# Issuing the main loop of a fused FFT-filter and MLP kernel in emission order

## The chip, the cores and the metric

The kernel runs on one core of one Trainium2 chip. The metric is the time of one execution in device microseconds (us), median of several runs. The profile is one execution taken by the hardware profiler. Engines are named as in it: PE is TensorE (PEld its weight loads), DVE VectorE, ACT ScalarE, POOL GpSimd, SP SyncE, which here does nothing but issue DMAs. The granted clock is the share of TensorE's full clock that the profile says it was given.

## The reference, cut to what matters

```python
X = np.fft.rfft(x, axis=1)                      # x: (8, 3008, 256)
y = np.fft.irfft(X * (filt_r + 1j * filt_i), n=3008, axis=1).astype(np.float32)
h = y.reshape(8 * 3008, 256) @ w_in             # (24064, 2048)
s = np.sin(alpha * h)
out = (h + s * s / (alpha + 1e-09)) @ w_out     # (24064, 256)
```

## The kernel before: the parts that matter

The Fourier filter is done per batch in three stages of small matmuls. They pass their data through DRAM tiles (d1, d2) to change its layout. Its pieces are emitted between the steps of the MLP loop by a plan, so that PE always has MLP work beside them. Loads and stores:

- stage 1: two `pa` matmuls a step, `t1` stored to d1; after the last, eight `t2` loads from d1;
- stage 2: `pb`, filter product `p`, `pc`, `g` stored to d2;
- stage 3: one `t4` load (384 KB) from d2 per chunk of four steps, then four `pd` matmuls a step, result `y`.

```python
xpool = pool("xp", 4)     # x, loaded on POOL's queue
t4pool = pool("t4", 3)
fps = pool("fps", 2, PSUM)     # pa, pb, pc, pd
hps = pool("hps", 4, PSUM)     # ph
ops = pool("ops", 2, PSUM)     # po
...
def stage3(u):                                  # u = 0..15, chunk ch = 0..3
    ch, rest = divmod(u, 4)
    half, cb = divmod(rest, 2)
    if rest == 0:
        t4 = t4pool.tile([NK, 8, C], FP16, name=f"t4_{b}_{ch}", tag="t4")
        marks["t4"] = nc.sync.dma_start(out=t4, in_=d2_rows[:, 8 * ch:8 * ch + 8, :])
        st["t4"] = t4
    ps = fps.tile([128, 4, 128], FP32, name=f"pd_{b}_{u}", tag="f")
    ...
    for i in range(4):
        nc.tensor.matmul(out=psv[:, i, :], lhsT=st["t4"][:, 4 * half + i, cb * 128:cb * 128 + 128],
                         rhs=wi_t, start=True, stop=True)                      # L219
    ...
...
plan = {1: [-45 + i for i in range(8)],
        2: [-29 + 14 * i / 13 for i in range(13)],
        3: [-10, -9] + [-7 + 2 * i for i in range(14)]}     # steps from 48 * b
...
for k in range(len(chunks) + 1):
    for j in range(8):                          # one step
        if k < len(chunks):
            hidden(k, 2 * j)                    # 2 ph matmuls (L354), sine on ACT, v on DVE
            hidden(k, 2 * j + 1)
        if k == 0:
            weights_out(j)
        while pending and pending[0][0] <= step:
            pending.pop(0)[2]()                 # the filter's pieces of this step
        if k > 0:
            n_half = 2 * (chunks[k - 1][2] // 128)
            for u in range(n_half * j // 8, n_half * (j + 1) // 8):
                project(k - 1, u)               # 8 po matmuls (L369); each 4th: ACT copies o, SP stores it
        step += 1
```

The Tile framework takes this program, finds the dependencies, and its scheduler chooses the order in which each engine's queue issues its instructions.

Of the kernel before, what the change touches and what calls it, by code (L numbers as in the profile page):

```python
# [12 lines left out]
ALU = mybir.AluOpType  # L13
# [41 lines left out]
def kernel(  # L55
# [10 lines left out]
    nc = tc.nc  # L66
# [12 lines left out]
    def behind(ins, other):  # L79

        tc.add_manual_dep(ins.ins, other.ins.name, mybir.DependencyInfo(
            mybir.DependencyClass.NoSync, mybir.DependencyReason.DATA), reason="order of work")
# [29 lines left out]
    marks = {}  # L112
# [158 lines left out]
    for g in range(4):  # L271
        for k, filt in enumerate((filt_r, filt_i)):
            for q in range(2):
                off, step = ((6 * g) * C, C) if q == 0 else ((N1 - 6 * g) * C, -C)
# [58 lines left out]
    def weights_out(i):  # L333

        if i in (2, 3, 4, 5):
            for jb in range(4 * i - 8, 4 * i - 4):
                behind(nc.vector.tensor_scalar(  # L337
                    out=w2[:, jb, :], in0=w_out32[:, jb, :], scalar1=rec_t[:, jb:jb + 1],
                    scalar2=-0.5, op0=ALU.mult, op1=ALU.mult), marks["snake"])


    chunks = [(pb, c0, min(512, 2 * S - c0)) for pb in range(B // 2) for c0 in range(0, 2 * S, 512)]
# [4 lines left out]
    def hidden(k, jb):  # L347

        _, c0, n = chunks[k]
        if jb == 0:  # L350
            v[k] = vpool.tile([128, 16, 512], FP16, name=f"v_{k}", tag="v")
        ps = hps.tile([128, 512], FP32, name=f"ph_{k}_{jb}", tag="h")
        for cb in range(2):
            nc.tensor.matmul(out=ps[:, 0:n], lhsT=w1[:, cb, jb * 128:jb * 128 + 128],  # L354
                             rhs=y_cols[:, cb, c0:c0 + n], start=(cb == 0), stop=(cb == 1))
        cs = cospool.tile([128, 512], FP32, name=f"cos_{k}_{jb}", tag="c")
        nc.scalar.activation(out=cs[:, 0:n], in_=ps[:, 0:n], func=AFT.Sin, bias=float(np.pi / 2))  # L357
        marks["snake"] = nc.vector.scalar_tensor_tensor(  # L358
            out=v[k][:, jb, 0:n], in0=cs[:, 0:n], scalar=-1.0, in1=ps[:, 0:n],
            op0=ALU.add, op1=ALU.subtract)  # L360

    def project(k, u):

        pb, c0, n = chunks[k]
        t, half = divmod(u, 2)
        if t % 2 == 0 and half == 0:
            pso[k] = ops.tile([128, 2, C], FP32, name=f"po_{k}_{t}", tag="o")
        for jb in range(8 * half, 8 * half + 8):
            nc.tensor.matmul(out=pso[k][:, t % 2, :], lhsT=v[k][:, jb, 128 * t:128 * t + 128],  # L369
                             rhs=w2[:, jb, :], start=(jb == 0), stop=(jb == 15))  # L370
        last = 128 * (t + 1) == n
        if half == 1 and (t % 2 == 1 or last):
            nb = t % 2 + 1
            o = opool.tile([128, 2, C], FP32, name=f"o_{k}_{t}", tag="o")
            nc.scalar.copy(out=o[:, 0:nb, :], in_=pso[k][:, 0:nb, :])  # L375
            for i in range(nb):
                store(o[:, i, :], pb, c0 + 128 * (t + 1 - nb + i))

    def store(o_blk, pb, col):

        p = 0
        while p < 128:
            odd, rest = divmod(col + p, S)
            n2, row = divmod(rest, NR)
            cnt = min(128 - p, NR - row)
            t0 = (2 * pb + odd) * S + 32 * row + n2
            nc.sync.dma_start(
                out=bass.AP(tensor=out.tensor, offset=out.offset + t0 * C,
                            ap=[[32 * C, cnt], [1, C]]),
                in_=o_blk[p:p + cnt, :])  # L390
            p += cnt
# [7 lines left out]
    pending = [(1 + i % 4 + 8 * (i // 4), 0, piece) for i, (_, piece) in enumerate(first[25:])]  # L399
# [7 lines left out]
            pending.append((at_step, b, piece))  # L407
    pending.sort(key=lambda p: p[0])
    step = 0
    for k in range(len(chunks) + 1):  # L410
        for j in range(8):
            if k < len(chunks):
                hidden(k, 2 * j)
                hidden(k, 2 * j + 1)
            if k == 0:
                weights_out(j)
            while pending and pending[0][0] <= step:
                pending.pop(0)[2]()
            if k > 0:
                n_half = 2 * (chunks[k - 1][2] // 128)  # L420
                for u in range(n_half * j // 8, n_half * (j + 1) // 8):
                    project(k - 1, u)
            step += 1



# [28 lines left out]
```

## Time and profile before

| | before |
|---|---|
| time, median of 4 runs (range) | 839.24 us (838.73 to 839.41) |
| PE busy / idle in the profiled span of 837.2 us | 799.8 / 37.4 us |
| PE's waits on t4 loads after 70 us | 1.6 us |
| mean granted TensorE clock | 0.988 |

From the page of the kernel before: PE's busy share, its busy tenths and its granted clock in 40 equal slices, the shares by engine of the chain that ended last, and two groups of instructions (count, busy us, mean ns, then the idle time just before them and what ended it).

```profile
PE 799.8 (96%) x5793; PEld 544.2 (65%) x5793; DVE 628.1 (75%) x1119; ACT 613.0 (73%) x1200; POOL 28.3 (3%) x55
...
PE   5758999999999999999999999999999999999996
...
PEclk9969999999999999999999999999999999999999
...
PE 83%; DMA 7%; ACT 4%; issue 3%; DVE 2%; POOL 0%; SPq 0%; ACTq 0%; DVEq 0%; POOLq 0%
...
L157 PE MATMUL pa<-x,wf_t 94*96 94x512 f16 x128 | 47.2, 408 | 10.1 <-DMA x<-in_x_dram 6.3
L219 PE MATMUL pd<-wi_t,t 96*128 96x94 f16 x512 | 43.4, 208 | 11.1 <-DMA t<-d 10.9
```

After a start of about 70 us PE is never free: the loop is bound by PE, and the 10.9 us that pd waits for t4 loads lie almost all in the start. Where the t4 loads stand on SP shows in the timeline of SP's queue (start us, duration us, what, count), here around the third stage of batch 3:

```profile
329.47 0.32 SPq L214 DMA_DIRECT2D t<-d  x1
330.24 1.79 SPq L387 DMA_DIRECT2D out_dram<-o  x5
332.07 0.78 SPq L214 DMA_DIRECT2D t<-d  x2
337.53 1.49 SPq L387 DMA_DIRECT2D out_dram<-o  x4
343.49 0.32 SPq L214 DMA_DIRECT2D t<-d  x1
...
382.42 5.33 SPq L169 DMA_DIRECT2D t<-d  x8
```

The durations are those of issuing only; where the data land is not in them (the Trainium skill, "Perfetto Trace Analysis", § DMA Instruction — HWDGE (DVE, Sync), says the same: the profiled window ends before the data movement does). The order of SP's list says that L214 at 329.47 is chunk 0, at 332.07 chunks 1 and 2, at 343.49 chunk 3. PE's timeline has the first pd of the four chunks at 333.76, 346.78, 362.44 and 380.29 us. The scheduler issued the last three loads 15, 30 and 37 us before their use, chunk 3's also ahead of the eight t2 loads of the next batch (L169).

### The profile page before, as it was taken

How to read it: one execution, taken by the hardware profiler on the slowest of the kernel's cores; microseconds unless marked ns; L12 is line 12 of the kernel's file. 1: busy time of each engine (PE TensorE's matmuls, PEld its weight loads, DVE VectorE, ACT ScalarE, POOL GpSimd, SP SyncE). 2: the span in 40 equal slices, each digit the busy share in tenths (PEclk: the TensorE clock that was granted, in tenths of full speed). 3: DMA queues.
4: the chain of work that ended last, by engine and by line, in shares of the span. 5: the costliest groups of instructions: out<-in, count | busy, mean ns of one | idle time of the engine just before them, and what ended most of it. 6: DMA issues, size and time to landing. Idle time of an engine off the chain costs nothing.

```text
span 837.2 us, 16122 instructions
## 1 busy us (share of the span) xinstructions
PE 799.8 (96%) x5793; PEld 544.2 (65%) x5793; DVE 628.1 (75%) x1119; ACT 613.0 (73%) x1200; POOL 28.3 (3%) x55
## 2 busy tenths in 40 slices
PE   5758999999999999999999999999999999999996
PEld 2425676667776677666776677666777677666674
DVE  3658886778877788777877788777877778777772
ACT  4536886787868787787877777777877878677763
POOL 3210000000000000000000000000000000000000
PEclk9969999999999999999999999999999999999999
DMA  9985835185344744266242763447443353421111
GB/s 220 218 255 117 200 89 130 51 174 116 82 135 81 171 99 109 75 141 153 65 130 60 165 137 82 115 91 171 92 96 94 97 113 83 115 58 38 38 40 45
DMA packets 93495, 94.98 MB, mean 113 GB/s; under 512 B 8084, under 2 KB 82852, under 8 KB 93416
## 3 DMA queue, kind: packets, MB, share of 16 engines
q1 hardware_dynamic: 84784, 75.02, 34.5%
q0 software_dynamic: 6704, 18.09, 12.5%
q10 hardware_dynamic: 1928, 0.86, 0.5%
q8 instruction: 45, 0.74, 0.3%
q14 instruction: 34, 0.28, 0.1%
HBM read 58.02 MB, written 49.81 MB: 129 GB/s over the span
## 4 chain that ended last, share of the span: by engine, by line
PE 83%; DMA 7%; ACT 4%; issue 3%; DVE 2%; POOL 0%; SPq 0%; ACTq 0%; DVEq 0%; POOLq 0%
PE po L369 36%; PE ph L354 35%; PE pc L199 4%; PE pa L157 3%; ACT cos L357 2%; PE pd L219 2%; PE pb L180 2%; DMA t<-d 1%; DMA w_out<-in_moe_w_out_dram 1%; DMA d<-g 1%; DMA d_t<-d_tbl 1%; DVE p L187 1%; DMA x<-in_x_dram 1%; DMA filt<-in_filt_i_dram 1%; ACT t L135 1%
## 5 line engine op out<-in xcount | busy, mean ns | idle before, releaser
L358 DVE SCALAR_TENSOR_TENSOR v<-cos,ph 128x512 f16<-128x512 f32 (+1 forms) x768 | 484.0, 672 | 164.0 <-ACT cos L357 163.5
L357 ACT ACTIVATE cos<-ph 128x512 f32<-128x512 f32 (+1 forms) x768 | 411.6, 589 | 153.9 <-PE ph L354 152.5
L369 PE MATMUL po<-w,v 128*128 128x256 f16 x3008 | 400.9, 273 | 2.6 <-DVE w L337 2.6
L354 PE MATMUL ph<-y,w 128*128 128x512 f16 (+1 forms) x1536 | 391.5, 377 | 0.2 <-ACT y L135 0.2
L369 PEld LDWEIGHTS <-v 128*128 128x128 f16 x3008 | 289.0, 98 | 80.9 <-issue 8.7
L354 PEld LDWEIGHTS <-w 128*128 128x128 f16 x1536 | 150.4, 98 | 101.0 <-issue 4.6
L187 DVE TENSOR_TENSOR p<-xf,filt 128x512 f16<-128x512 f16 x192 | 72.1, 419 | 4.9 <-ACT xf L183 4.5
L375 ACT COPY o<-po 128x512 f32<-128x512 f32 x96 | 55.6, 579 | 17.7 <-PE po L369 15.5
L135 ACT CAST t<-pa 96x512 f16<-96x512 f32 x89 | 51.0, 589 | 19.0 <-PE pa L157 18.9
L183 ACT CAST xf<-pb 128x512 f16<-128x512 f32 x96 | 57.0, 595 | 8.1 <-PE pb L180 5.5
L219 PEld LDWEIGHTS <-t 96*128 96x128 f16 x512 | 36.3, 100 | 39.8 <-DMA t<-d 11.8
L199 PE MATMUL pc<-p,e_t 128*128 128x256 f16 x384 | 59.7, 275 | 2.6 <-DVE p L187 1.5
L157 PE MATMUL pa<-x,wf_t 94*96 94x512 f16 x128 | 47.2, 408 | 10.1 <-DMA x<-in_x_dram 6.3
L219 PE MATMUL pd<-wi_t,t 96*128 96x94 f16 x512 | 43.4, 208 | 11.1 <-DMA t<-d 10.9
L135 ACT CAST y<-pd 128x376 f16<-128x376 f32 x82 | 39.1, 479 | 12.5 <-PE pd L219 12.5
L199 PEld LDWEIGHTS <-e_t 128*128 128x128 f16 x384 | 37.6, 99 | 15.6 <-issue 7.1
L180 PE MATMUL pb<-t,d_t 128*128 128x256 f16 x192 | 38.2, 283 | 2.5 <-DMA t<-d 1.5
L135 ACT CAST g<-pc 128x512 f16<-128x512 f32 x64 | 38.7, 605 | 1.6 <-PE pc L199 1.6
L137 DVE CAST t<-pa 96x512 f16<-96x512 f32 x39 | 26.6, 683 | 15.8 <-PE pa L157 15.8
L180 PEld LDWEIGHTS <-d_t 128*128 128x128 f16 x192 | 18.9, 101 | 23.8 <-issue 4.6
L118 POOL DMA_DIRECT2D x<-in_x_dram x32 | 16.7, 524 | 502.8 <-PE pa L157 490.5
L157 PEld LDWEIGHTS <-wf_t 94*96 94x96 f16 x128 | 16.6, 129 | 19.6 <-issue 9.9
(28 smaller groups left out, 94.3 us busy)
## 6 DMA issues: line engine op xcount, KB each, us to landing
d<-t SPq DMA_DIRECT2D x32, 384.0 KB
d<-g SPq DMA_DIRECT2D x64, 192.0 KB
t<-d SPq DMA_DIRECT2D x32, 384.0 KB
x<-in_x_dram POOLq DMA_DIRECT2D x32, 376.0 KB, 6.9
t<-d SPq DMA_DIRECT2D x60, 192.0 KB
out_dram<-o SPq DMA_DIRECT2D x72, 94.0 KB
w_in<-in_moe_w_in_dram POOLq DMA_DIRECT2D x2, 1024.0 KB, 9.2
w_out<-in_moe_w_out_dram POOLq DMA_DIRECT2D x1, 2048.0 KB, 11.6
```

Of the source, the lines that this page charges most:

```text
L135: marks["act"] = nc.scalar.copy(out=dst, in_=src)
L157: marks["pe"] = nc.tensor.matmul(out=ps[0:NK, :], lhsT=wf_t, rhs=st["x"][ch][:, n0:n0 + 2, :], start=True, stop=True)
L180: nc.tensor.matmul(out=ps[:, i, :], lhsT=d_t[:, s, :], rhs=st["t2"][s // 6][:, s % 6, :], start=True, stop=True)
L183: nc.scalar.copy(out=xf, in_=ps)
L187: marks["prod", u] = nc.vector.tensor_tensor(out=pt, in0=xf, in1=f_t[k][:, 2 * u:2 * u + 2, :], op=ALU.mult)
L199: nc.tensor.matmul(out=ps[:, i, :], lhsT=e_t[:, k, 2 * w + i, :], rhs=pr[k][:, i, :], start=(k == 0), stop=(k == 1))
L219: nc.tensor.matmul(out=psv[:, i, :], lhsT=st["t4"][:, 4 * half + i, cb * 128:cb * 128 + 128], rhs=wi_t, start=True, stop=True)
L354: nc.tensor.matmul(out=ps[:, 0:n], lhsT=w1[:, cb, jb * 128:jb * 128 + 128], rhs=y_cols[:, cb, c0:c0 + n], start=(cb == 0), stop=(cb == 1))
L357: nc.scalar.activation(out=cs[:, 0:n], in_=ps[:, 0:n], func=AFT.Sin, bias=float(np.pi / 2))
L358: marks["snake"] = nc.vector.scalar_tensor_tensor(out=v[k][:, jb, 0:n], in0=cs[:, 0:n], scalar=-1.0, in1=ps[:, 0:n], op0=ALU.add, op1=ALU. ...
L369: nc.tensor.matmul(out=pso[k][:, t % 2, :], lhsT=v[k][:, jb, 128 * t:128 * t + 128], rhs=w2[:, jb, :], start=(jb == 0), stop=(jb == 15))
L375: nc.scalar.copy(out=o[:, 0:nb, :], in_=pso[k][:, 0:nb, :])
```

## The change

The intent: the plan above was written so that each step has a good mix of work; `manual_schedule` makes every engine issue the loop exactly as the plan emits it. No instruction is added or removed, and the two `behind` lines go because the order now says the same.

```diff
         if i in (2, 3, 4, 5):
             for jb in range(4 * i - 8, 4 * i - 4):
-                behind(nc.vector.tensor_scalar(
+                nc.vector.tensor_scalar(
                     out=w2[:, jb, :], in0=w_out32[:, jb, :], scalar1=rec_t[:, jb:jb + 1],
-                    scalar2=-0.5, op0=ALU.mult, op1=ALU.mult), marks["snake"])
+                    scalar2=-0.5, op0=ALU.mult, op1=ALU.mult)
@@
     step = 0
-    for k in range(len(chunks) + 1):
-        for j in range(8):
-            ... (the body, as above)
+    with tc.manual_schedule():
+        for k in range(len(chunks) + 1):
+            for j in range(8):
+                ... (the same body)
```

More of the change, by code (lines that the diff above doesn't have):

```diff
@@ L409 @@
     step = 0
-    for k in range(len(chunks) + 1):
-        for j in range(8):
-            if k < len(chunks):
-                hidden(k, 2 * j)
-                hidden(k, 2 * j + 1)
-            if k == 0:
-                weights_out(j)
-            while pending and pending[0][0] <= step:
-                pending.pop(0)[2]()
-            if k > 0:
-                n_half = 2 * (chunks[k - 1][2] // 128)
-                for u in range(n_half * j // 8, n_half * (j + 1) // 8):
-                    project(k - 1, u)
-            step += 1
+    with tc.manual_schedule():
+        for k in range(len(chunks) + 1):
+            for j in range(8):
+                if k < len(chunks):
+                    hidden(k, 2 * j)
+                    hidden(k, 2 * j + 1)
+                if k == 0:
+                    weights_out(j)
+                while pending and pending[0][0] <= step:
+                    pending.pop(0)[2]()
+                if k > 0:
+                    n_half = 2 * (chunks[k - 1][2] // 128)
+                    for u in range(n_half * j // 8, n_half * (j + 1) // 8):
+                        project(k - 1, u)
+                step += 1
 _INS = ['x', 'filt_r', 'filt_i', 'moe_w_in', 'moe_w_out', 'moe_alpha']
```

## The prediction

> **What bounds the kernel now.** The page gives PE 96% busy (799.8 of 837.2 us), DVE 75%, ACT 73%. The chain of waits that ended last is 83% PE. PE's own waits in the whole trace sum to about 30 us, nearly all before 66 us; from there the loop is one unbroken PE stream. A better order can win a few us; any new PE stall adds directly.
>
> **What the change does.** No instruction is added or removed. PE, ACT and DVE get them step by step: two hidden pairs (ph), a DFT piece, one half projection (8 po). POOL's x loads still run a batch ahead. What matters is SP: before, the loads t4 (the third stage's input, 384 KB) stood two together, far ahead of their users (3 buffers). Now each stands where it was emitted, in the same piece as the pd matmuls that read it, behind output stores, and PE is in order and must wait for it.
>
> **Cost, from the trace.** A plain step on PE is 0.86 us (ph) + 0.88 us (po x8) = 1.74 us. Output copy 0.58 us; five stores issue in 1.8 us; a t4 load took 3.98 us from issue to landing; eight t2 loads take 5.3 us to issue; SP waits about 3.5 us for a d1 write before them.
> - Chunk 1 and 2 of each batch: last store is two steps earlier. Landing 0.65+1.8+4.0 = 6.5 us after that step; PE arrives after 1.74+0.86 = 2.6 us: stall about 4 us each (chunk 2 follows a d1 write instead, about the same).
> - Chunk 0: one step more room: about 2.3 us.
> - Chunk 3: behind the last d1 write of the next batch (issued 3 us into its step), its landing (3.3), eight t2 loads (5.3), stores (2.5), load (4): lands at 18 us, PE arrives at 7: stall about 11 us. (Estimates all.)
> Sum: about 22 us per batch for batches 1-6, 11 for batch 0, 14 for the last: about 157 us.
> - Steps with both a pd and two pa pieces need three buffers of a two-buffer pool (fps): about 0.8 us, 24 times: 19 us.
> - Second-stage steps: DVE (2x0.67+2x0.42+evictions) about equals PE's 2.4 us; product-to-pc margin 0.2 us: 8 us in all.
> - Clock: the Trainium skill, "TensorE: Matmul & The Clock Gate", Part 1, says that an idle window of about 3.4 us halves PE's clock and about as long a busy one restores it. The trace agrees: in the windows at 48-52 us PE is empty and the clock granted 0.50, still 0.50 for 52-58. The 11 us stalls should each cost about 2 us more, the 4 us ones sometimes: 17 us.
> - Filling the first chunk: 3 us.
>
> All of it is on the critical path, as PE is. Gain: at most 3 us.
>
> **Prediction:** 839 + about 204 = 1043 us; range 965 to 1100. Faster by 2%: 0.01; within 2%: 0.03; slower: 0.96.
>
> **What would show it.** PE waits, L219 (pd, matmul and weight load) on DMA t<-d: from 23 us to 120-180 us, about 28 times, seven of them near 10 us; pa waits on ACT/DVE t or y about 20 us; PE's busy sum rises little; PE share falls to about 80%; slices with clock under 9 appear about once a batch; DVE and ACT busy time unchanged.
>
> **What would make it wrong.** SP running further ahead than I think (stores released earlier), so the stalls shrink: about 930. Second-stage stalls much larger than costed: above 1100. If t4 loads still land before pd, the time stays at 840.

## The result, and the profile after

| | before | after |
|---|---|---|
| time, median of 4 runs (range) | 839.24 us | 1131.95 us (1128.84 to 1139.51) |
| profiled span | 837.2 us | 1127.0 us |
| PE busy / idle | 799.8 / 37.4 us | 856.2 / 270.8 us |
| PE's waits on t4 loads after 70 us | 1.6 us | 208.4 us |
| mean granted clock | 0.988 | 0.882 |

The ratio is 1.350 (95% interval 1.344 to 1.357). Here and below a ratio is the mean time of one kernel's runs over that of the other's of the same rounds, so it is not quite the ratio of the medians. The change is slower by far, and by more than predicted. The page of the changed kernel, the same lines as before:

```profile
PE 856.2 (76%) x5793; PEld 564.0 (50%) x5793; DVE 631.8 (56%) x1119; ACT 619.3 (55%) x1200; POOL 28.1 (2%) x55
...
PE   5573978649986498864996759877499667978896
...
PEclk8687998879988799987998869988699888989999
...
PE 58%; DMA 21%; DVE 6%; ACT 6%; SPq 4%; issue 4%; DVEq 0%; ACTq 0%; POOLq 0%
...
L219 PE MATMUL pd<-wi_t,t 96*128 96x94 f16 x512 | 46.8, 221 | 216.8 <-DMA t<-d 216.5
...
L157 PE MATMUL pa<-x,wf_t 94*96 94x512 f16 x128 | 51.2, 445 | 25.7 <-ACT t L135 9.0
```

The span grew by 289.8 us: PE's idle time by 233.4 and its busy time by 56.4. Of the idle time, 206.8 us (208.4 less 1.6) is pd waiting for t4 loads in the loop. The slices show holes in PE once per batch and, behind each, a lower clock. The four waits of one batch in PE's timeline (batch 2; the bracket is the idle time before the instruction and what ended it):

```profile
309.69 0.34 PE L219 MATMUL pd<-wi_t,t 96*128 96x94 f16 x4 [1.88 <-DMA t<-d]
326.56 0.49 PE L219 MATMUL pd<-wi_t,t 96*128 96x94 f16 x4 [5.14 <-DMA t<-d]
350.09 0.50 PE L219 MATMUL pd<-wi_t,t 96*128 96x94 f16 x4 [6.56 <-DMA t<-d]
387.33 0.49 PE L219 MATMUL pd<-wi_t,t 96*128 96x94 f16 x4 [15.10 <-DMA t<-d]
```

By chunk, added up over all batches from 70 us on: chunk 0 21.4 us (7 waits), chunk 1 31.1 (7), chunk 2 44.5 (7), chunk 3 106.8 (7, 12.9 to 17.3 each) and 4.6 in the last batch, which has no next batch to load for. That is the 208.4 us. There are 29 such waits, 26 of them over 3.3 us.

Why chunk 3 is the worst is seen in SP's timeline of the changed kernel (batch 1) and in the chain of waits of the same stretch. First SP, then the chain:

```profile
226.41 5.66 SPq L161 DMA_DIRECT2D d<-t  x2
237.95 5.34 SPq L169 DMA_DIRECT2D t<-d  x8
243.39 1.98 SPq L387 DMA_DIRECT2D out_dram<-o  x5
245.76 0.32 SPq L214 DMA_DIRECT2D t<-d  x1
```

```profile
231.74 6.07 DMA d<-t
...
241.33 4.37 DMA t<-d
...
245.76 5.50 DMA t<-d
251.32 0.49 PE pd L219 x4
```

PE had run out of work at 235.4 us. The load it needs stood in SP's queue behind the next batch's last d1 write (landing after 6.07 us), eight t2 loads that wait for this write, and five stores; it was issued at 245.76 and landed 5.5 us later. None of what stood ahead of it has anything to do with it. PE issues in the order of its list, so the po matmuls behind the pd had to wait with it.

### The profile page after: what moved, and what is told of

Same layout as the page of the kernel before. It is cut to its first block, busy times and chain, and to the rows that moved or that the text cites. A ratio compares the mean times of both kernels' runs of the same rounds, so it can differ in the third digit from the quotient of the medians.

```text
span 1127.0 us, 16145 instructions
## 1 busy us (share of the span) xinstructions
PE 856.2 (76%) x5793; PEld 564.0 (50%) x5793; DVE 631.8 (56%) x1119; ACT 619.3 (55%) x1200; POOL 28.1 (2%) x55
## 4 chain that ended last, share of the span: by engine, by line
PE 58%; DMA 21%; DVE 6%; ACT 6%; SPq 4%; issue 4%; DVEq 0%; ACTq 0%; POOLq 0%
PE po L369 27%; PE ph L354 23%; DMA t<-d 15%; DMA d<-t 3%; ACT cos L357 3%; PE pc L199 3%; PE pa L157 3%; SPq L169 3%; DVE v L358 2%; PE pd L219 2%; DVE p L187 2%; SPq L387 2%; DVE g L137 1%; ACT t L135 1%; PE pb L180 1%
## 5 line engine op out<-in xcount | busy, mean ns | idle before, releaser
L369 PE MATMUL po<-w,v 128*128 128x256 f16 x3008 | 419.0, 286 | 0.0
L354 PE MATMUL ph<-y,w 128*128 128x512 f16 (+1 forms) x1536 | 411.2, 393 | 6.0 <-DVE v L358 5.0
L369 PEld LDWEIGHTS <-v 128*128 128x128 f16 x3008 | 303.1, 102 | 110.2 <-issue 35.4
L354 PEld LDWEIGHTS <-w 128*128 128x128 f16 x1536 | 156.8, 102 | 119.7 <-issue 27.2
L219 PE MATMUL pd<-wi_t,t 96*128 96x94 f16 x512 | 46.8, 221 | 216.8 <-DMA t<-d 216.5
L157 PE MATMUL pa<-x,wf_t 94*96 94x512 f16 x128 | 51.2, 445 | 25.7 <-ACT t L135 9.0
L137 DVE CAST y<-pd 128x376 f16<-128x376 f32 x46 | 25.0, 544 | 70.6 <-PE pd L219 70.6
L183 ACT CAST xf<-pb 128x512 f16<-128x512 f32 x96 | 57.0, 595 | 10.2 <-PE pb L180 7.3
```

The lines of the kernel that those rows point to most:

```text
L137: marks["dve"] = nc.vector.tensor_copy(out=dst, in_=src)
L157: marks["pe"] = nc.tensor.matmul(out=ps[0:NK, :], lhsT=wf_t, rhs=st["x"][ch][:, n0:n0 + 2, :], start=True, stop=True)
L183: nc.scalar.copy(out=xf, in_=ps)
L354: nc.tensor.matmul(out=ps[:, 0:n], lhsT=w1[:, cb, jb * 128:jb * 128 + 128], rhs=y_cols[:, cb, c0:c0 + n], start=(cb == 0), stop=(cb == 1))
L369: nc.tensor.matmul(out=pso[k][:, t % 2, :], lhsT=v[k][:, jb, 128 * t:128 * t + 128], rhs=w2[:, jb, :], start=(jb == 0), stop=(jb == 15))
```

## The experiments

Ten kernels were run, each with a correct result; all are timed beside the kernel before on their chip. The table is for overview; the column "t4 waits" is PE's total waiting for t4 loads in pd, the start of the kernel (8 to 10.5 us) included.

| run | what it is | median us | ratio to before | t4 waits us | clock |
|---|---|---|---|---|---|
| before | | 839.24 | 1 | 10.9 | 0.988 |
| after | manual on all engines | 1131.95 | 1.350 | 216.5 | 0.882 |
| e1_sp_free | manual, but SP scheduled | 876.86 | 1.043 | 15.8 | 0.980 |
| e2_sp_only | manual on SP alone | 912.76 | 1.086 | 61.6 | 0.968 |
| e3_early4 | t4 loads emitted 4 steps early | 881.95 | 1.049 | 16.6 | 0.982 |
| e3_early2 | t4 loads emitted 2 steps early | 989.66 | 1.175 | 111.1 | 0.936 |
| e7_ch3_early | only chunk 3's loads, 4 steps early | 1005.27 | 1.196 | 109.5 | 0.930 |
| e8_t4_pool | t4 loads issued by POOL | 893.41 | 1.062 | 29.9 | 0.975 |
| e9_t2_pool | t2 loads issued by POOL | 1058.89 | 1.258 | 147.3 | 0.916 |
| e4_x_later | x loads released later | 1107.04 | 1.316 | 195.1 | 0.892 |
| e5_dummy | PE kept busy while it waits | 1099.67 | 1.306 | 67.4 | 0.962 |
| e6_split | repaired version | 844.70 | 1.005 | 14.6 | 0.980 |

### Which engine's order costs: SP's, or that of the compute engines

`manual_schedule` can be given a set of engines. Two runs take the change apart: e1 leaves SP to the scheduler, e2 takes SP alone.

```diff
-    with tc.manual_schedule():
+    with tc.manual_schedule(engines={mybir.EngineType.PE, mybir.EngineType.Activation,   # e1
+                                     mybir.EngineType.DVE, mybir.EngineType.Pool}):
+    with tc.manual_schedule(engines={mybir.EngineType.SP}):       # e2; the behind lines put back
```

> The manual order on PE, ACT, DVE and POOL, with SP's queue left to the scheduler. The built program's PE and ACT lists are the same as those of the changed kernel, line for line; only SP's differs (t4 loads up to two or three chunks ahead). Theory A, the position of the t4 loads on SP is the cause: pd waits on DMA t<-d fall from 216 us to under 25, what stays is the pool wait of pa (18 us) and pc (8 us): 855 to 875 us. Rival B, the compute engines' own emission order costs: over 950 us.

Measured: 876.86 us, ratio 1.043 (1.041 to 1.044). PE's waits in this run, longest in total first (total us, times, longest):

```profile
PE pd L219 <- DMA t<-d: 15.8, 2, 10.1
PE pa L157 <- ACT t L135: 11.1, 16, 1.1
PE pa L157 <- ACT y L135: 9.8, 14, 0.7
PE ph L354 <- DVE v L358: 6.8, 4, 5.2
...
PE pc L199 <- DVE g L137: 5.7, 23, 0.3
```

With PE, ACT and DVE in exactly the order of the changed kernel (the two traces list the same 5793 matmuls and the same ACT and DVE instructions in the same order), and only SP's list different, 255 of the 293 us are gone. The order of the compute engines by itself costs the rest, about 37 us; this is 2 us above the expected range. The rival, that the compute engines' order makes most of the loss, is refuted.

> The manual order on SP alone; SP's list is the same as that of the changed kernel, PE, ACT and DVE are the scheduler's. In the built program the scheduler now puts the first pd of a chunk 3: 13.5 us of PE work later than in the changed kernel, the others 1.3 to 5.5 us later. Theory A as I predicted with (a late load stalls PE whatever else): over 1100 us. Theory A2 (a late load costs only because PE may not go on with other work): stalls fall to the wait less this shift, about 7 us per batch, and the clock stays near 1.0: 870 to 920 us.

Measured: 912.76 us, ratio 1.086 (1.081 to 1.092). SP's list is the same as in the changed kernel (630 DMAs in the same order in both traces), yet 219 of the 293 us are gone. PE's wait in this run:

```profile
PE pd L219 <- DMA t<-d: 61.6, 25, 8.2
```

So most of the loss needs both: a late load, and a PE that may not take other work first. The scheduler moved the first pd of a chunk behind more ph and po work, by up to 13.5 us of it in the built program. The form of the theory with which I had predicted, that a late load stalls PE whatever else, is too strong. It holds in full only where PE's order is fixed too.

### How early, and past what

e3 emits each t4 load as a piece of its own, some steps before its first pd, in manual order on all engines.

```diff
-            if rest == 0:
-                t4 = ...; marks["t4"] = nc.sync.dma_start(...)
+        def load_t4(ch): ...                     # the same two lines
+        for ch in range(4):
+            pieces.append((4, lambda ch=ch: load_t4(ch)))
@@ plan, lead 4 (lead 2: -12, -5, 3, 11)
+            4: [-14, -7, 1, 9]}
```

> Manual order on all engines as in the changed kernel, but each t4 load emitted as a piece of its own four steps before its first pd (chunk 0 of batch 1: two steps). Theory A: the waits on t4 go nearly to nothing, 850 to 880 us, granted clock over 0.97. If four steps (about 8 us) are too few for chunk 3 or the store queue ahead of it: up to 930. Rival B: over 950.

Measured: 881.95 us, ratio 1.049 (1.046 to 1.052), slightly over the upper end of the range. The waits on t4 are 16.6 us, those of e1. A first build of this version: in batch 1 the load stood ahead of the last writes to d2, that is, it read memory that was not yet written. A load that is moved up by hand needs its producer looked up by hand; batch 1 got a lead of two steps.

> All t4 loads emitted two steps early in place of four; manual order on all engines. In SP's list this puts the loads of chunks 1 and 2 ahead of the stores that they stood behind, leaves chunk 0 behind the same stores, and leaves chunk 3 behind the eight t2 loads, only ahead of the five stores after them. Theory A in its queue form (a load is as early as what stands ahead of it on SP, whatever the lead in steps): chunks 1 and 2 stall under 1 us, chunk 0 stays at 1.9 to 3.4 us, chunk 3 falls only by the 2.1 us of the stores, to 12 to 13.5 us; 985 to 1010 us in all. If the lead in time is what counts (two steps are 4 us off each stall): chunk 0 goes to 0, chunks 1 and 2 to 1 to 3 us, chunk 3 to about 11 us.

Measured: 989.66 us, ratio 1.175 (1.171 to 1.179), clock 0.936. Two steps of lead for all chunks, and the chunks answer differently. Two waits of batch 3 in PE's timeline, chunk 0 and chunk 3 (chunks 1 and 2 do not appear, they no longer wait):

```profile
395.53 0.49 PE L215 MATMUL pd<-wi_t,t 96*128 96x94 f16 x4 [3.65 <-DMA t<-d]
460.73 0.50 PE L215 MATMUL pd<-wi_t,t 96*128 96x94 f16 x4 [13.44 <-DMA t<-d]
```

Chunk 0 waits as before (1.9 to 3.7 us in batches 2 to 7), for the same stores still stand ahead of it on SP. Chunk 3 waits 12.7 to 13.6 us in batches 1 to 5, about 2 us less than before, which is the time of the five stores that it passed; the t2 loads still stand ahead of it. In batch 6 it falls by about as much, from 12.9 to 10.6 us; in batch 0, where two steps take the load past the t2 loads and the last d1 write as well, from 17.3 to 1.5 us. The queue form of the theory holds: a load gains what it is moved past on SP, not the steps by which it is emitted earlier.

e7 moves only chunk 3's load, by four steps, which is past the last d1 write and the t2 loads of the next batch:

```diff
@@ plan of the t4 loads
-            4: [-10, -3, 5, 13]}     # as in the changed kernel
+            4: [-10, -3, 5, 9]}
```

> The changed kernel with only the chunk 3 loads emitted four steps earlier, which puts them ahead of the last d1 write and the eight t2 loads of the next batch on SP; all else as in the changed kernel. Theory A: chunk 3's seven long stalls (107 us in all, the stall of the last batch not counted) go, and with them about 2 us of clock each: 1000 to 1025 us. If a chunk 3 load only costs what any late load costs (5 us each): over 1080 us.

Measured: 1005.27 us, ratio 1.196 (1.192 to 1.201), in the expected range. Chunk 3's waits in the batches with a next batch fall from 106.8 to 4.2 us in all, the last batch's 4.6 us goes too, those of chunks 0 to 2 stay as they were. PE's wait in this run:

```profile
PE pd L215 <- DMA t<-d: 109.5, 26, 9.1
```

Chunk 3 alone made 127 of the 293 us.

### Whether it is the queue, or the place in the emission order

e8 issues the t4 loads on POOL's queue, at the same place of the emission order; e9 leaves them on SP and takes the t2 loads of batches 1 to 7 out of their way.

```diff
-                marks["t4"] = nc.sync.dma_start(out=t4, ...)
+                marks["t4"] = nc.gpsimd.dma_start(out=t4, ...)          # e8
-                        eng = nc.scalar if b == 0 and p else nc.sync
+                        eng = nc.gpsimd if b else nc.scalar if p else nc.sync    # e9
```

> The changed kernel with the t4 loads issued by POOL in place of SP, at the same place of the emission order; PE's list is unchanged. Theory A in its narrow form, it is the stores, d1 writes and t2 loads ahead of them on SP's queue that make the t4 loads late, not the place in the emission order: POOL's queue runs ahead, pd waits nearly vanish, 865 to 890 us. If POOL's queue holds them up as well (x loads ahead of them that wait for buffers): over 950 us.

Measured: 893.41 us, ratio 1.062 (1.059 to 1.064), 3 us over the range. One word changed, and 239 us are gone. On POOL only x loads stand near the t4 loads, and the trace shows them issued there without a wait, four in 2.08 us; no store, d1 write or t2 load stands ahead of a t4 load any more. PE's wait in this run:

```profile
PE pd L219 <- DMA t<-d: 29.9, 7, 9.0
```

A side effect: the x loads now stand behind the t4 loads of chunks 0 and 1, so a part of the gain may be theirs; e4 below gives 25 us for holding them back alone. That POOL is somewhat slower for this (29.9 us of waits against 15.8 in e1, all in chunk 0) goes with the landing times listed for its queue, 6.2 us for a t4 load; I did not follow this further.

> The changed kernel with the t2 loads of batches 1 to 7 issued by POOL in place of SP; the t4 loads stay on SP at their place of the emission order and PE's list is unchanged. Theory A, chunk 3's stall is long because SP must first wait for the d1 write to land and issue eight t2 loads: it falls from 15.3 to the 4 to 7 us of chunks 1 and 2, and the time to 1050 to 1075 us. Rival, the t2 loads' bytes (1.5 MB) on the DMA engines are what delays it: 8 to 12 us stay, 1085 to 1110 us. (x loads then stand behind the t2 loads on POOL, as a side effect, and leave the d1 and chunk 2 loads alone.)

Measured: 1058.89 us, ratio 1.258 (1.255 to 1.262), in the range of theory A. Chunk 3's wait of batch 2 in this run, for the 15.10 us shown above:

```profile
353.57 0.49 PE L219 MATMUL pd<-wi_t,t 96*128 96x94 f16 x4 [6.10 <-DMA t<-d]
```

In batches 1 to 6 chunk 3 now waits 5.4 to 7.3 us. In the changed kernel's batch 2, PE ran out of work at 372.2 us and the load was issued 8.5 us later, at 380.77; here PE ran out at 347.5 and the load had been issued at 346.98. From issue to pd both took 6.6 us, here with the eight t2 loads going out on POOL from 347.03 on. So the part of the stall that went was the place in SP's queue, and not bandwidth; what the load would lose behind bytes already under way is not tested by this run. (The x loads came to stand behind the t2 loads on POOL in this run, so a part of the gain in chunk 2 is theirs, see next.)

### Why the waits were longer than predicted

The prediction had 4 us for chunk 2 and 11 us for chunk 3, against 6.4 and 15.3 us measured. In the chain above two terms are larger than those I had put in: the d1 write landed after 6.07 us (I had 3.3), the t4 load after 5.50 (I had 4.0). e4 tests whether x loads, which POOL issues as soon as a pa frees its buffer, are the reason: it holds them until a t4 load of a quieter time.

```diff
-            if b == 1:
+            if b >= 1:
                 after(ins, marks["t4"])
```

> The changed kernel with each batch's x loads held until the t4 load of chunk 1 of the batch before has landed, which takes them out of the time of the d1, t2 and chunk 2 and 3 loads. Theory C, the stalls are longer than predicted (15.5 for 11 us in chunk 3, 6.6 for 4 us in chunk 2) because x loads share the DMA engines: chunk 3 stalls fall to about 12 us, chunk 2 to about 5, sum of pd waits from 216 to about 185, time 1085 to 1105 us. Rival: x loads do not matter, time within 1125 to 1140.

Measured: 1107.04 us, ratio 1.316 (1.312 to 1.321), 2 us over the range. The waits fall by 21 us: chunk 2's by 10.6, chunk 3's by 13.5 (six of seven are shorter, by 0.9 to 3.5 us, one is 0.3 us longer), while those of the start grow by 1.7. The chain of waits at chunk 3 of batch 2, first in the changed kernel, then in this run:

```profile
368.09 5.38 DMA d<-t
...
380.77 6.52 DMA t<-d
387.33 0.49 PE pd L219 x4
```

```profile
359.51 2.97 DMA d<-t
...
369.87 6.45 DMA t<-d
376.37 0.50 PE pd L219 x4
```

The d1 write lands 2.4 us sooner, and the wait of PE is shorter by the same (12.71 for 15.10 us). The t4 load is as slow as before. So in this batch the x loads explain the first term and not the second. That the t2 loads, in flight just ahead of the t4 load, explain the second is likely but not shown: in the changed kernel a chunk 3 load took 4.9 to 6.6 us from issue to pd in the seven batches with t2 loads of a next batch, 4.7 in the last, which has none; in e9, with the t2 loads beside it, 5.5 to 8.3.

### The clock

PE's busy time rose by 56 us though its work is the same. e5 fills the waits with matmuls whose result is overwritten, so that PE waits without being idle.

```diff
+            if rest == 0 and (b, ch) not in ((0, 0), (0, 1), (0, 2)):
+                for _ in range((8, 16, 16, 60 if b < 7 else 16)[ch]):
+                    nc.tensor.matmul(out=ps.rearrange("p a b -> p (a b)"), lhsT=d_t[:, 0, :],
+                                     rhs=e_t[:, 0, 0:4, :], start=True, stop=True)
             for i in range(4):
                 nc.tensor.matmul(out=psv[:, i, :], ...
```

> The changed kernel with useless matmuls (128x512, their result is overwritten) ahead of the first pd of each chunk, 8, 16, 16 and 60 of them, sized to fill about 160 of the 208 us in which PE waits for t4, so that PE is not idle while it waits. Theory D, the idle PE loses its clock and the 52 us by which PE's busy time grew (856 against 804 us in the run with SP free) are that loss: the clock granted rises from 0.88 to over 0.97 and the time falls to 1075 to 1095 us although PE is given 160 us of extra work. Rival, PE's growth in busy time is an artefact or has another cause: the time stays at 1125 to 1140 us.

Measured: 1099.67 us, ratio 1.306 (1.301 to 1.311). PE has 172 us more busy time than in e1 and the kernel is 32 us faster than the changed one. The same place in both, in windows: start and end us, their length, busy us of PE, PEld, DVE, ACT and POOL (with counts), granted clock, DMA share, GB/s. First the changed kernel, then e5:

```profile
235.00:251.00 16.00, 0.38 (x2) 0.00 (x0) 1.50 (x3) 1.07 (x2) 0.00 (x0) 0.65 0.69 154
251.00:257.00 6.00, 5.68 (x25) 3.46 (x26) 1.38 (x2) 1.67 (x3) 0.00 (x0) 0.51 0.01 1
```

```profile
235.00:248.00 13.00, 10.58 (x49) 4.61 (x47) 0.00 (x0) 0.00 (x0) 0.00 (x0) 1.00 0.81 171
248.00:254.00 6.00, 5.66 (x45) 3.97 (x46) 2.90 (x5) 3.41 (x7) 0.00 (x0) 1.00 0.01 1
```

In the 6 us after the wait, the changed kernel does 25 matmuls at clock 0.51, e5 45 at 1.00. The direction is shown; the gain of 32 us is below the 37 to 57 expected, and the mean clock rose to 0.962, not over 0.97. The filler was shorter than many waits (67 us of idle remain), so not all of the loss was taken back; it may also have run past some load, which costs. That leaves 32 us as what the run shows of the clock's part, and PE's growth in busy time (856.2 against 803.9 us in e1, where the same instructions run at clock 0.980) of 52 us as the larger reading of it. The clock records of the traces speak for the larger: after 70 us PE was busy at half clock for 115.8 us in the changed kernel, 10.9 in e1 and 44.4 in e5 (filler included). Half of the difference to e1 is 52 us, and half of that to e5 is 36 us, near the 32 us gained; both halves are estimates, as if each matmul took twice as long at half clock.

Which waits cost clock: after batch 2's wait of 1.88 us the granted clock stayed 1.00 (309.7 to 313 us), after the wait of 5.14 us it was 0.50 (326.6 to 330), and after one of 3.36 us 0.54 (720.9 to 724). So nearly every wait of chunks 1 and 2 cost clock too, not only the long ones. Of the 26 waits of more than 3.3 us, 25 did, down to one of 3.33 us; one of 3.44 us (batch 7) did not, and the clock stayed 1.00. So the length alone does not decide:

```profile
445.33 0.50 PE L219 MATMUL pd<-wi_t,t 96*128 96x94 f16 x4 [3.33 <-DMA t<-d]
1033.58 0.34 PE L219 MATMUL pd<-wi_t,t 96*128 96x94 f16 x4 [3.44 <-DMA t<-d]
```

The half-clock stretches last 3.4, 6.8, 10.2, 13.7 or 17.1 us, whole multiples of 3.41 us. 52 us over the 26 waits is 2.0 us each.

### What is left, and a version without it

e6 keeps the manual order from the third 512-column chunk on, but leaves SP and the start to the scheduler. It moves the second pa of a step and the pc behind the po matmuls, and batch 1's second stage one step up.

```diff
+    manual = {PE, Activation, DVE, Pool}
+        with tc.manual_schedule(engines=manual) if k >= 2 else ExitStack():
@@ in a step
                 while pending and pending[0][0] <= step:
-                    pending.pop(0)[2]()
+                    late.append(pending.pop(0)[2]())    # returns its second half, if it has one
                 ... project ...
+                for piece in late:
+                    if piece is not None:
+                        piece()
```

> A version meant to be as fast as the kernel before: SP and the first two chunks of the loop left to the scheduler, the rest in manual order, with the second pa of a step and the four pc moved behind the half projection, and the second stage of batch 1 one step earlier. Theory E, what is left of the loss with SP free (877 against 840 us) is the wait of pa for a third buffer of a pool of two (23 us), pc on DVE (6 us), the start of the loop (ph on DVE v, 7 us) and one late load (6 us): pa and pc waits go to under 5 us and the time is 838 to 850 us. If the residue is elsewhere: 865 to 880.

Measured: 844.70 us, ratio 1.005 (1.002 to 1.007): the same as the kernel before within 2%, in the expected range. The waits of pa on ACT and DVE in the loop fall from 23.5 us in e1 (11.1 + 9.8 + 2.6) to 3.7 us (2.6 + 1.1), those of pc on DVE's g go:

```profile
PE pa L163 <- DVE t L137: 2.6, 5, 0.8
PE pc L212 <- DVE p L195: 2.0, 4, 0.8
PE pa L163 <- ACT t L135: 1.1, 5, 0.2
```

Several things were changed at once here, so the run says that they together close the rest, not which part each has. No version beat the kernel before: PE was already busy 96% of its span.

## Why the prediction was right or wrong

The direction, the mechanism and the place were right; the time, 1043 us (965 to 1100), was too low: 1131.95 us were measured. Point by point:

- "PE's own waits ... nearly all before 66 us; ... any new PE stall adds directly": right. PE's idle time grew by 233 us, and the span by 290.
- "What matters is SP": right, shown by e1 (SP free: ratio 1.043) and by e8 (another queue: 1.062). Not seen in advance: fixing SP alone costs only a ratio of 1.086 (e2), as the scheduler lets PE take other work. The loss is that of both orders together.
- **"lands at 18 us, PE arrives at 7: stall about 11 us" and "stall about 4 us each"; "Sum: ... about 157 us"**: this term was mis-sized. It measured 208 us: chunk 3 15.3 us on average for 11, chunk 2 6.4 for 4, chunk 1 4.4 for 4, chunk 0 3.1 for 2.3. I had taken a landing time of 3.3 us for the d1 write and 4.0 for the t4 load; in the chain of batch 1 they took 6.07 and 5.50. The 4.0 is the load at 48.22 us of the trace before, where the DMA engines were 0.69 busy: it was not a quiet moment, so that traffic as such explains the difference is not shown. e4 shows that x loads are the reason for the first (and for about 23 of the 51 us of waits in the loop); for the second the reason is open.
- **"The 11 us stalls should each cost about 2 us more, the 4 us ones sometimes: 17 us"**: also mis-sized. It measured between 32 us (e5) and 52 us (PE's busy time against e1). The Trainium skill, "TensorE: Matmul & The Clock Gate", Part 1, gives an idle window of about 3.4 us for the clock to halve; this agrees closely (1.88 us cost nothing, 3.33 us already cost, though one wait of 3.44 did not). The 2 us for each stall were right; their number was not. I had counted seven and a few of the rest, and 25 lost clock.
- "fps ... 19 us" and second stage "8 us": the sizes were right. pa waited 18.9 us on ACT and DVE after evictions t and y (9.0 + 8.5 + 1.4), pc 7.5 us; but 5.7 of these were for DVE's eviction g and only 1.8 for the product, of which 1.5 were there before.
- "PE's busy sum rises little": wrong, by 56 us, with the clock. "PE share falls to about 80%": 76%.
- "about 28 times, seven of them near 10 us": 29 in the loop, seven of 12.9 to 17.3 us.

The two mis-sized terms, 51 us of waits and 15 to 35 us of clock, are 66 to 86 of the 89 us by which the prediction missed.

## What to carry to other kernels

A DMA queue that is issued in order is a line of waits: a load is as early as the slowest thing ahead of it, whatever the lead at which it was emitted, so before fixing an order, look at what each load stands behind on its queue, move it past the stores and the chained loads, or give it a queue of its own (one word, 1132 to 893 us). An order that was good under a scheduler carries its prefetching in the scheduler, not in the text; when fixing it, fix the compute engines if you like, but emit loads apart from their users. When costing a stall, take landing times from a stage with the same traffic (a d1 write took 5.38 us beside x loads and 2.97 without), and count a PE wait of more than about 3.3 us as costing some 2 us of clock on top (25 of 26 such waits did here; waits of 1.9 us did not).

## What the Trainium skill lacked or had wrong

- "DMA: Bandwidth & Descriptors", § Issuing engines are not separate DMA queues: it says that issuing from several engines only saves the sequencer's issue time, usually small. Here the same loads, issued by POOL in place of SP, took 239 us off (e8), and moving the t2 loads 73 us (e9), a part of each perhaps through the x loads: what was saved is in the main the waits of unrelated DMAs ahead in the same queue. The page lacks this.
- "TensorE: Matmul & The Clock Gate", Part 1: the window of about 3.4 us fits here, as the half-clock stretches of 3.4 to 17.1 us are whole multiples of 3.41. Not on the page: waits a little shorter than a window cost clock (3.33, 3.36 and 3.39 us) and one of 3.44 did not; and the clock can fall after the wait has ended. After a wait of 3.36 us the first pd group still ran at full speed (0.34 us), while the granted clock from its start to 3 us later was 0.54.
- No page has a landing time under the load of other transfers for DMAs of this size ("DMA: Bandwidth & Descriptors", § Latency and other measured facts, has only an HBM access latency that grows with load): a 384 KB write to DRAM landed after 2.97 us without the x loads and after 5.38 us with them.
